# Weights masked on VectorE instead of ScalarE, and products with v moved behind the transposes, in a fused attention and feed-forward kernel

## The chip, the cores and the metric

The kernel runs on one core of one Trainium2 chip. The metric is the device time of a whole execution in microseconds (us), as the median of several. TensorE multiplies matrices (its weight loads are listed apart), VectorE, ScalarE and GpSimd do the element-wise work, and SyncE issues most transfers. The profile calls them PE, PEld, DVE, ACT, POOL and SP.

## The reference

```python
# q, k, v: (8, 8, 576, 64) float32; tau = 0.02
scores = np.matmul(q, k.transpose(0, 1, 3, 2)) / 8
thresh = scores.max(-1, keepdims=True) - tau
scores = np.where(scores >= thresh, scores, -1e9)
attn = np.exp(scores - scores.max(-1, keepdims=True))
attn = attn / (attn.sum(-1, keepdims=True) + 1e-9)
x = heads_joined(np.matmul(attn, v))                  # (8, 576, 512)
xn = (x - x.mean(-1)) / np.sqrt(x.var(-1) + 1e-6) * g_ln
out = x + np.maximum(xn @ w_ch1, 0) @ w_ch2           # w: 512x2048 and 2048x512
```

(cut; the keepdims of the second block are left out.) The weights come in 64-bit floating point and are made into 32-bit ones on the chip.

## The kernel before

The work is a chain of 160 steps. Eight batches have four pairs of heads each, and a pair has five steps (places 0 to 4 in the pair): four with 128 rows of each head, one with the last 64 rows of both. A step is: scores on TensorE, row maximum on VectorE (`neg`), threshold on GpSimd (`thr`), exponential on ScalarE, mask by the threshold and row sum on VectorE (`e`), reciprocal on VectorE (`den`), scaling on GpSimd. A step or two later the weights of attention are transposed and multiplied with v (`pv`). In the first batch (steps 0 to 19) TensorE transposes; in the others VectorE transposes 32x32 blocks (`et`), a transfer writes them to DRAM (`scr`) and another fetches them back in the right order (`em`).

Up to step 27 the kernel also converts the weights, one chunk of 128x512 a step and two in steps 20 to 23. The bits of a chunk are put together in `a`; `y` is a factor that is 0 where the weight is too small for a 32-bit number, and otherwise 1 or the feature's g:

```python
nc.scalar.activation(y, high_words_as_f32, func=AF.Square)
gh = half_sb if gi is None else g_half[:, gi : gi + 1]
nc.scalar.activation(y, y, func=AF.Sign, bias=tiny_sb)
nc.scalar.activation(y, y, func=AF.Identity, scale=gh, bias=gh)
...                                                   # in the next step:
nc.gpsimd.tensor_tensor(out=chunks[i][0], in0=a, in1=y, op=ALU.mult)
```

From step 25 on the feed-forward products of the batch before (`p`, 2304 matmuls in all) fill the time between the attention steps. The transposes and the order of the first batch:

```python
def turn_weights(u, j, es):
    ...
    tr = ps_at.tile([128, 2, 128], F32, tag="at", name="tr")   # two PSUM buffers "at"
    for h in range(2):
        tp = pool.tile([128, J, 128], F32, tag=tag, name="tp") # "at" for h == 0
        ...                              # 4 transposes into tp, then em <- tp on ScalarE
    for h in range(2):
        ...
        nc.vector.tensor_copy(er[r, o : o + 128], tr[r, h])    # the last 64 rows

at_point(3 * n + 3, turn_weights, u, j, es)      # next step, behind its scores
if j in (1, 3, 4):                               # the step after, ahead of its transposes
    at_point(3 * n + 6, lambda u=u, j=j: values_of(u, j, rounds.pop(u)))
```

`values_of` takes an "at" buffer for the products with v and copies the result to `x` on ScalarE. In the batches 1 to 7 it is called at `3 * n + 12`, four steps after the scores.

Of the kernel before, what the change touches and what calls it, by code (L numbers as in the profile page):

```python
# [8 lines left out]
F32 = mybir.dt.float32  # L9
# [3 lines left out]
ALU = mybir.AluOpType  # L13
AF = mybir.ActivationFunctionType
# [4 lines left out]
def kernel(  # L19
# [25 lines left out]
    nc = tc.nc  # L45
# [5 lines left out]
    NK = DM // 128  # L51
# [11 lines left out]
    consts = ctx.enter_context(tc.tile_pool(name="consts", bufs=1))  # L63
# [13 lines left out]
    low_sb = consts.tile([128, 1], F32, name="low_sb")  # L77
    eps_sb = consts.tile([128, 1], F32, name="eps_sb")
    g_sb = consts.tile([128, NK], F32, name="g_sb")
    g_half = consts.tile([128, NK], F32, name="g_half")  # L80
    half_sb = consts.tile([128, 1], F32, name="half_sb")
    tiny_sb = consts.tile([128, 1], F32, name="tiny_sb")
    ident = consts.tile([128, 128], F32, name="ident")
    avg_sb = consts.tile([128, 128], F32, name="avg_sb")
    w1_sb = [consts.tile([128, DF], F32, name=f"w1_{i}") for i in range(NK)]
# [26 lines left out]
    def load_v(u):  # L112
# [13 lines left out]
        out=tau_sb, in_=bass.AP(tensor=tau.tensor, offset=tau.offset, ap=[[0, 128], [1, 1]])  # L126
# [3 lines left out]
    for t in q_diag:  # L130
# [3 lines left out]
    make_identity(nc, ident)  # L134
    nc.vector.memset(eps_sb, 1e-6)
    nc.vector.memset(avg_sb, 1.0 / DM)
    nc.vector.memset(half_sb, 0.5)
    nc.vector.memset(tiny_sb, -(1.0625 * 2.0**-15) ** 2)



# [1 line left out]
        out=scl_sb, in0=tau_sb, scalar1=0.0, scalar2=SCALE, op0=ALU.is_ge, op1=ALU.mult  # L143
    )
    nc.vector.tensor_scalar(
        out=low_sb, in0=tau_sb, scalar1=0.0, scalar2=BIG, op0=ALU.is_lt, op1=ALU.mult
    )
    nc.vector.scalar_tensor_tensor(
        out=low_sb, in0=tau_sb, scalar=-1.0, in1=low_sb, op0=ALU.mult, op1=ALU.subtract
    )  # L150
    nc.gpsimd.dma_start(out=g_sb, in_=g_ln.rearrange("(c p) -> p c", p=128))
    nc.gpsimd.tensor_scalar(
        out=g_half, in0=g_sb, scalar1=0.5, scalar2=1.0, op0=ALU.mult, op1=ALU.mult
    )

    WC = 512

# [2 lines left out]
    def weight_steps(which):  # L160










        if which == 1:
            chunks = [
                (w1_sb[i][:, c : c + WC], w_ch1[i * 128 : (i + 1) * 128, c : c + WC], i)
                for c in range(0, DF, WC)
                for i in range(NK)
            ]
        else:
            chunks = [
                (w2_sb[i], w_ch2[i * 128 : (i + 1) * 128, :], None) for i in range(ND)
            ]  # L180
        size = len(chunks)
        step = 4 if which == 1 else 2
        place = [ND - step * ((i % 4 if which == 1 or i < size - 4 else i % 2) + 1) for i in range(size)]
        raws, made = {}, {}

        def fetch_raw(i):
            at = place[i]
            raws[i] = hidden[:, at : at + 2].rearrange("p a n -> p (a n)").bitcast(I64)
            nc.sync.dma_start(out=raws[i], in_=chunks[i][1])

        def begin(i):
            if which == 1:
                a, y = hidden[:, place[i] + 2], hidden[:, place[i] + 3]
            else:
                a = ffn.tile([128, WC], F32, tag="o", name="w_bits")
                y = ffn.tile([128, WC], F32, tag="o", name="w_size")
            raw = raws.pop(i)
            words = raw.bitcast(U32).rearrange("p (n two) -> p n two", two=2)
            lo, hi = words[:, :, 0], words[:, :, 1]
            r = raw.bitcast(I32).rearrange("p (n two) -> p n two", two=2)[:, :, 0]  # L200
            au = a.bitcast(U32)
            nc.vector.tensor_scalar(
                out=au, in0=hi, scalar1=3, scalar2=0x3FFFFFFF,
                op0=ALU.logical_shift_left, op1=ALU.bitwise_and,
            )
            nc.vector.scalar_tensor_tensor(
                out=au, in0=hi, scalar=0xC0000000, in1=au,
                op0=ALU.bitwise_and, op1=ALU.bitwise_or,
            )
            nc.scalar.activation(r, lo, func=AF.Copy, scale=2.0**-29)  # L210
            nc.scalar.activation(
                y, raw.bitcast(F32).rearrange("p (n two) -> p n two", two=2)[:, :, 1],
                func=AF.Square,
            )
            gi = chunks[i][2]
            gh = half_sb if gi is None else g_half[:, gi : gi + 1]
            nc.scalar.activation(y, y, func=AF.Sign, bias=tiny_sb)
            nc.scalar.activation(y, y, func=AF.Identity, scale=gh, bias=gh)
            made[i] = (a, y, r)

        def carry(i):
            a, y, r = made[i]
            ai = a.bitcast(I32)
            nc.gpsimd.tensor_tensor(out=ai, in0=ai, in1=r, op=ALU.add)
            if place[i] in place[i + 1 :]:
                fetch_raw(place.index(place[i], i + 1))

        def end(i):
            a, y, r = made.pop(i)
            nc.gpsimd.tensor_tensor(out=chunks[i][0], in0=a, in1=y, op=ALU.mult)  # L230

        return size, lambda: [fetch_raw(place.index(at)) for at in sorted(set(place), reverse=True)], begin, carry, end

    def by_blocks(u):

        return units[u][0] > 0
# [83 lines left out]
    rounds = {}  # L320

    def turn_weights(u, j, es):


        if j in (0, 2, 4):
            n = 256 if j < J else 64
            em = att.tile([128, 2, J, 256], F32, tag="em", name="em")
            er = att.tile([128, 256], F32, tag="er", name="er")
            rounds[u] = (em, er, n)
        em, er, n = rounds[u]  # L330
        tr = ps_at.tile([128, 2, 128], F32, tag="at", name="tr")
        for h in range(2):
            e = es[:, h] if j < J else es[:, 0]
            if j < J or h == 0:
                pool, tag = (ps_at, "at") if h == 0 else (ps_ff, "ff")
                tp = pool.tile([128, J, 128], F32, tag=tag, name="tp")
                for c in range(J):
                    nc.tensor.transpose(tp[:, c], e[:, c * 128 : (c + 1) * 128], ident)  # L338
                if j < J:
                    o = (j % 2) * 128  # L340
                    nc.scalar.copy(em[:, h, :, o : o + 128], tp)
                else:
                    nc.scalar.copy(
                        em[:, :, :, :64], tp.rearrange("p c (h t) -> p h c t", h=2)
                    )
            if h == 0:
                nc.tensor.transpose(tr[:64, 0], e[:, 512:576], ident)
            else:
                nc.tensor.transpose(tr[:, 1], e[:, 448:576], ident)
        for h in range(2):  # L350
            r = slice(64 * h, 64 * h + 64)
            if j < J:
                o = (j % 2) * 128
                nc.vector.tensor_copy(er[r, o : o + 128], tr[r, h])
            else:
                nc.vector.tensor_copy(er[r, :64], tr[r, h, r])

    def turn_blocks(u, j, es):

# [102 lines left out]
    def run_aside():  # L462
        now = aside[:]
        aside.clear()
        for fn in now:
            fn()
# [124 lines left out]
    def at_point(n, fn, *args):  # L591
        later_calls.setdefault(n, []).append((fn, args))

    def run(n):
        for fn, args in later_calls.pop(n, ()):
            fn(*args)
# [47 lines left out]
    n = 0  # L644
    for u in range(len(units)):
        for j in range(PTS):
            blocks = by_blocks(u)
            scs = scores(u, j)
            es, thr = exponentials(scs)
            conversion.carry()  # L650
            run(3 * n)
            second_part(n, 0)
            weights(scs, es, thr)
            run_aside()
            conversion.end()
            run(3 * n + 1)
            second_part(n, 1)
            if j == 2 and u + 1 < len(units):
                turn(u + 1)
            if j == 3 and u + 2 < len(units):  # L660
                load_qk(u + 2)
            if j == 4 and 0 < u < len(units) - 1:
                load_v(u + 1)
            conversion.begin(2 if 20 <= n < 24 else 1)
            if blocks:
                box = []
                at_point(3 * n + 4, lambda u=u, j=j, es=es, box=box: box.append(turn_blocks(u, j, es)))
                if j in (1, 3, 4):
                    at_point(3 * n + 7, lambda j=j, box=box: box.append(fetch(j, box[0])))
                    at_point(3 * n + 12, lambda u=u, j=j, box=box: values_of(u, j, box[1]))  # L670
            else:
                at_point(3 * n + 3, turn_weights, u, j, es)
                if j in (1, 3, 4):
                    at_point(3 * n + 6, lambda u=u, j=j: values_of(u, j, rounds.pop(u)))
            n += 1
    while later_calls or queue or aside:
        run(3 * n)
# [35 lines left out]
```

## Time and profile before

| | |
|---|---|
| median of 3 executions | 1567.52 us (1562.31 to 1567.53) |
| profiled execution | 1561.5 us, mean granted clock 0.965 |
| PE busy | 95% of the span |
| VectorE, ScalarE, GpSimd busy | 52%, 30%, 33% |

The prediction shows the views that it rests on. Four more lines of the page of before turn out to matter. The first is the chain that ended last, by engine. The second is the group of the products with v: busy time and mean ns of one, then the idle time of TensorE just before them and what ended it. The last two are transfers: count, KB each, and median us from issue to landing.

```profile
PE 79%; SPq 6%; DVE 5%; DMA 4%; POOL 2%; ACT 2%; issue 2%; POOLq 0%; DVEq 0%; ACTq 0%
...
L416 PE MATMUL pv<-em,v_in 128*64 128x256 f32 (+1 forms) x1536 | 167.1, 353 | 6.1 <-DMA em<-scr 5.9
...
scr<-et SPq DMA_DIRECT2D x224, 288.0 KB, 4.4
em<-scr SPq DMA_DIRECT2D x112, 512.0 KB, 5.0
```

The products with v lose only 6.1 us to waiting, so the fetch of `em` looks harmless. But it is there (5.9 us), in the dense part of the kernel, where TensorE is the bound, and 10% of the chain (SP's queue and DMA) are transfers.

### The profile page before, as it was taken

To read this page: it belongs to the slowest core of one execution; us is meant where nothing else is said; L and a number is where in the kernel's file an instruction comes from. 1 tells how busy PE (TensorE), PEld (TensorE's weight loads), DVE (VectorE), ACT (ScalarE), POOL (GpSimd) and SP (SyncE) were. 2 spreads that over 40 slices of the span, in tenths; PEclk is the share of its full clock that TensorE was granted. 3 is DMA by queue.
4 is the path that set the end of the run, shared out by engine and by line. 5 is a ranking of instruction groups with operands and counts; after the bars stand their busy time and mean duration, and the time that the engine had idled before them with its cause. 6 is when DMAs were issued, how large, how long until landed. Compare 5 with 4: busy or idle time off the path is not lost.

```text
span 1561.5 us, 17868 instructions
## 1 busy us (share of the span) xinstructions
PE 1477.1 (95%) x5686; PEld 714.8 (46%) x5686; DVE 808.6 (52%) x1548; ACT 460.8 (30%) x786; POOL 513.9 (33%) x774
## 2 busy tenths in 40 slices
PE   5777699999999999999999999999999999999998
PEld 3444344444444444444444444444444444444443
DVE  5666676666556655665566555655656551001001
ACT  5666664212321232123211421133113320210200
POOL 4656673333223322333233323332333222100000
PEclk8867599999999999999999999999999999999999
DMA  5333387787667776777667767776777665001001
GB/s 141 96 87 94 106 199 165 166 182 163 152 156 173 165 167 152 161 152 190 141 150 167 162 156 159 157 174 150 159 154 169 149 139 121 7 3 17 7 7 20
DMA packets 701452, 204.37 MB, mean 131 GB/s; under 512 B 632752, under 2 KB 697264, under 8 KB 701360
## 3 DMA queue, kind: packets, MB, share of 16 engines
q1 hardware_dynamic: 698960, 202.95, 57.1%
q8 instruction: 46, 0.75, 0.2%
q10 hardware_dynamic: 2368, 0.30, 0.1%
q14 instruction: 46, 0.38, 0.1%
q0 software_dynamic: 32, 0.00, 0.0%
HBM read 119.41 MB, written 83.76 MB: 130 GB/s over the span
## 4 chain that ended last, share of the span: by engine, by line
PE 79%; SPq 6%; DVE 5%; DMA 4%; POOL 2%; ACT 2%; issue 2%; POOLq 0%; DVEq 0%; ACTq 0%
PE p L494 31%; PE p L536 26%; PE pv L416 10%; PE sc L278 10%; DMA em<-scr 4%; DVE e L309 2%; SPq L103 2%; SPq L479 1%; SPq L372 1%; ACT e L297 1%; PE tp L338 1%; SPq L117 1%; DVE neg L290 1%; SPq L121 1%; POOL w L230 1%
## 5 line engine op out<-in xcount | busy, mean ns | idle before, releaser
L494 PE MATMUL p<-xc,w 128*128 128x512 f32 x1152 | 518.6, 600 | 12.5 <-DVE xc L455 9.8
L536 PE MATMUL p<-hidden,w 128*128 128x512 f32 x1152 | 513.1, 597 | 0.0
L297 ACT ACTIVATE e<-sc,neg 128x576 f32<-128x576 f32 x288 | 199.9, 737 | 602.7 <-DVE neg L290 588.5
L290 DVE TENSOR_REDUCE neg<-sc 128x1 f32<-128x576 f32 x288 | 206.2, 751 | 309.7 <-PE sc L278 309.0
L494 PEld LDWEIGHTS p<-xc,w 128*128 128x128 f32 x1152 | 213.1, 190 | 270.0 <-issue 244.9
L536 PEld LDWEIGHTS p<-hidden,w 128*128 128x128 f32 x1152 | 214.2, 190 | 263.2 <-issue 260.5
L315 POOL TENSOR_SCALAR e<-e,den 128x576 f32<-128x576 f32 x288 | 218.3, 764 | 257.1 <-DVE den L313 241.1
L309 DVE SCALAR_TENSOR_TENSOR e<-sc,thr,e 128x576 f32<-128x576 f32 x288 | 225.4, 816 | 70.4 <-ACT e L297 69.0
L293 POOL TENSOR_SCALAR thr<-neg,low_sb 128x1 f32<-128x1 f32 x288 | 76.0, 264 | 501.2 <-DVE neg L290 500.3
L278 PE MATMUL sc<-kT,qT 64*128 64x288 f32 x1024 | 188.3, 459 | 39.4 <-DVE e L309 30.9
L501 ACT ACTIVATE hidden<-p 128x512 f32<-128x512 f32 x144 | 86.0, 598 | 352.6 <-PE p L494 352.5
L416 PE MATMUL pv<-em,v_in 128*64 128x256 f32 (+1 forms) x1536 | 167.1, 353 | 6.1 <-DMA em<-scr 5.9
L278 PEld LDWEIGHTS sc<-kT,qT 64*128 64x128 f32 x1024 | 103.2, 198 | 148.8 <-issue 93.7
L365 DVE STREAM_TRANSPOSE et<-e 128x1152 f32<-128x1152 f32 x112 | 152.9, 1365 | 0.5
L416 PEld LDWEIGHTS pv<-em,v_in 128*64 128x64 f32 x1536 | 93.6, 145 | 85.4 <-issue 43.4
L471 POOL TENSOR_TENSOR o<-o,x 128x512 f32<-128x512 f32 x36 | 45.7, 1268 | 216.5 <-DVE o L470 216.5
L470 DVE TENSOR_TENSOR o<-p,rb 128x512 f32<-128x512 f32 x36 | 24.6, 683 | 161.5 <-PE p L536 150.0
L416 PE MATMUL pv<-er,v_rest 128*64 128x256 f32 (+1 forms) x384 | 54.3, 332 | 0.0
L510 POOL TENSOR_TENSOR ss<-ss,sq 128x512 f32<-128x512 f32 x27 | 34.4, 1273 | 60.1 <-ACT sq L508 60.1
L427 ACT COPY x<-pv 128x256 f32<-128x256 f32 (+3 forms) x120 | 32.0, 288 | 46.3 <-PE pv L416 42.9
L278 PE MATMUL sc<-kT,q_diag 128*128 128x288 f32 x128 | 37.7, 418 | 6.3 <-DVE e L309 6.2
L255 DVE STREAM_TRANSPOSE qT<-q_in 128x256 f32<-128x256 f32 x56 | 21.6, 423 | 41.6 <-POOL q_in L248 41.6
(68 smaller groups left out, 694.6 us busy)
## 6 DMA issues: line engine op xcount, KB each, us to landing
scr<-et SPq DMA_DIRECT2D x224, 288.0 KB, 4.4
em<-scr SPq DMA_DIRECT2D x112, 512.0 KB, 5.0
hidden<-in_moe_w_ch_dram SPq DMA_DIRECT2D x32, 512.0 KB, 3.8
q_in<-in_q_dram SPq DMA_DIRECT2D x128, 72.0 KB, 4.3
out_dram<-ot SPq DMA_DIRECT2D x144, 64.0 KB, 1.9
k_in<-in_k_dram SPq DMA_DIRECT2D x124, 72.0 KB, 2.6
v_in<-in_v_dram SPq DMA_DIRECT2D x64, 128.0 KB, 3.6
scr_rest<-et SPq DMA_DIRECT2D x112, 72.0 KB, 4.6
```

Of the source, the lines that this page charges most:

```text
L278: nc.tensor.matmul(sc[:, c, :HALF], lhsT=lhsT, rhs=kT[rows, c * HALF : (c + 1) * HALF], start=True, stop=True,)
L290: nc.vector.tensor_reduce(out=neg[:, i : i + 1], in_=sc[:, :, :HALF], axis=AXL.XY, op=ALU.max, negate=True)
L293: nc.gpsimd.tensor_scalar(out=thr[:, i : i + 1], in0=neg[:, i : i + 1], scalar1=-1.0, scalar2=low_sb, op0=ALU.mult, op1=ALU.add,)
L297: nc.scalar.activation(es[:, i].rearrange("p (c n) -> p c n", c=2), sc[:, :, :HALF], func=AF.Exp, bias=neg[:, i : i + 1],)
L309: nc.vector.scalar_tensor_tensor(out=e2, in0=sc[:, :, :HALF], scalar=thr[:, i : i + 1], in1=e2, op0=ALU.is_ge, op1=ALU.mult, accum_out=den ...
L315: nc.gpsimd.tensor_scalar(out=es[:, i], in0=es[:, i], scalar1=den[:, i : i + 1], scalar2=1.0, op0=ALU.mult, op1=ALU.mult,)
L365: nc.vector.transpose(et[:, :, :, j % 2], es.rearrange("p h (n c) -> p h n c", c=32))
L416: nc.tensor.matmul(pv[64 * h : 64 * h + 64, :n], lhsT=vt[:, c, h, :] if c < J else vr[:, h, :], rhs=em[:, h, c, :n] if c < J else er[:, :n ...
L471: nc.gpsimd.tensor_tensor(out=o, in0=o, in1=groups[g][:, m], op=ALU.add)
L494: nc.tensor.matmul(p1, lhsT=w1_sb[c][:, d * 128 : (d + 1) * 128], rhs=xc[:, c, :], start=(c == 0), stop=(c == NK - 1),)
L501: nc.scalar.activation(hidden[:, d], p1, func=AF.Relu)
L536: nc.tensor.matmul(p2, lhsT=w2_sb[d][:, m * 128 : (m + 1) * 128], rhs=hidden[:, d], start=(d == 0), stop=(d == ND - 1),)
```

## The change

The intent: ScalarE's two operations Sign and Identity go, as does GpSimd's multiplication. VectorE does test and multiplication in one instruction. GpSimd then scales by g, for the first matrix only. In the first batch the products with v are issued half a step later, behind the transposes, and the `er` copies go to ScalarE.

```diff
-    g_half = consts.tile([128, NK], F32, name="g_half")
-    half_sb = consts.tile([128, 1], F32, name="half_sb")
-    tiny_sb = consts.tile([128, 1], F32, name="tiny_sb")
 ...
-            gi = chunks[i][2]
-            gh = half_sb if gi is None else g_half[:, gi : gi + 1]
-            nc.scalar.activation(y, y, func=AF.Sign, bias=tiny_sb)
-            nc.scalar.activation(y, y, func=AF.Identity, scale=gh, bias=gh)
 ...
-            nc.gpsimd.tensor_tensor(out=chunks[i][0], in0=a, in1=y, op=ALU.mult)
+            dst, _, gi = chunks[i]
+            nc.vector.scalar_tensor_tensor(
+                out=dst if gi is None else a, in0=y, scalar=(1.0625 * 2.0**-15) ** 2, in1=a,
+                op0=ALU.is_ge, op1=ALU.mult,
+            )
+            if gi is not None:
+                nc.gpsimd.tensor_scalar(
+                    out=dst, in0=a, scalar1=g_sb[:, gi : gi + 1], scalar2=1.0,
+                    op0=ALU.mult, op1=ALU.mult,
+                )
 ...
-                nc.vector.tensor_copy(er[r, o : o + 128], tr[r, h])
+                nc.scalar.copy(er[r, o : o + 128], tr[r, h])
 ...
-                    at_point(3 * n + 6, lambda u=u, j=j: values_of(u, j, rounds.pop(u)))
+                    at_point(3 * n + 7, lambda u=u, j=j, tw=rounds_at: values_of(u, j, tw[0]))
```

(cut: the filling of the removed constants, the other `er` copy, the list that carries `em` and `er` to the later point.)

More of the change, by code (lines that the diff above doesn't have):

```diff
@@ L136 @@
     nc.vector.memset(avg_sb, 1.0 / DM)
-    nc.vector.memset(half_sb, 0.5)
-    nc.vector.memset(tiny_sb, -(1.0625 * 2.0**-15) ** 2)
     nc.vector.tensor_scalar(
@@ L151 @@
     nc.gpsimd.dma_start(out=g_sb, in_=g_ln.rearrange("(c p) -> p c", p=128))
-    nc.gpsimd.tensor_scalar(
-        out=g_half, in0=g_sb, scalar1=0.5, scalar2=1.0, op0=ALU.mult, op1=ALU.mult
-    )
     WC = 512
@@ L353, in turn_weights @@
                 o = (j % 2) * 128
-                nc.vector.tensor_copy(er[r, o : o + 128], tr[r, h])
+                nc.scalar.copy(er[r, o : o + 128], tr[r, h])
             else:
-                nc.vector.tensor_copy(er[r, :64], tr[r, h, r])
+                nc.scalar.copy(er[r, :64], tr[r, h, r])
+        return em, er, n
     def turn_blocks(u, j, es):
@@ L671 @@
             else:
-                at_point(3 * n + 3, turn_weights, u, j, es)
+                rounds_at = []
+                at_point(
+                    3 * n + 3,
+                    lambda u=u, j=j, es=es, tw=rounds_at: tw.append(turn_weights(u, j, es)),
+                )
                 if j in (1, 3, 4):
-                    at_point(3 * n + 6, lambda u=u, j=j: values_of(u, j, rounds.pop(u)))
+                    at_point(3 * n + 7, lambda u=u, j=j, tw=rounds_at: values_of(u, j, tw[0]))
             n += 1
```

## The prediction

> **What bounds the kernel now.** I read the busy shares by slices of the span first, then stretches cut at the first score reduction of each pair of heads, then the chain that ended last in order of time, then the order of instructions inside single steps.
>
> The page, busy tenths in 40 slices of 39 us, and the granted clock in tenths:
>
> ```profile
> PE   5777699999999999999999999999999999999998
> PEclk8867599999999999999999999999999999999999
> ```
>
> After slice 5 (about 200 us) TensorE is busy nine tenths or more at full clock; only the first 200 us are loose. The same as stretches (PE, PEld, DVE, ACT, POOL busy us, clock, DMA share, GB/s), one pair of heads of the first batch each, then the steps in which two chunks of weights are converted, then the beginning of the dense part:
>
> ```profile
> 44.80:81.20 36.40, 26.36 (x141) 16.11 (x138) 25.45 (x58) 25.15 (x42) 23.89 (x30) 0.78 0.35 91
> 81.20:122.20 41.00, 31.11 (x150) 19.04 (x150) 25.86 (x58) 24.96 (x42) 25.16 (x31) 0.70 0.33 90
> 122.20:159.50 37.30, 27.27 (x139) 17.18 (x136) 25.43 (x58) 25.23 (x42) 24.97 (x31) 0.74 0.32 90
> 159.50:215.00 55.50, 38.43 (x132) 18.40 (x132) 38.09 (x67) 33.92 (x54) 36.28 (x40) 0.68 0.53 143
> 215.00:260.00 45.00, 45.00 (x193) 21.87 (x190) 31.65 (x59) 26.64 (x45) 25.47 (x34) 1.00 0.79 183
> ```
>
> Before 215 us no engine is full, so the limit there is a cycle of waits. After it PE is full, so what is won before 215 us stays won and what is won after it is worth nothing. All that the change touches (32 chunks in steps 0 to 27, the transposes in steps 1 to 20) lies before about 240 us. The chain that ended last shows the cycle in one step (start, us, what):
>
> ```profile
> 88.42 3.02 PE sc L278 x8
> 91.44 1.26 PE pv L416 x20
> 92.70 1.05 PE tp L338 x4
> 93.97 0.85 PE tp L338 x4
> 95.36 0.29 DVE er L354
> 95.69 0.84 DVE e L309 x2
> 96.57 3.02 PE sc L278 x8
> ```
>
> Scores, then the previous products with v, then the previous transposes, then VectorE's copy of the last rows (er). Only behind that copy, in VectorE's order, stands the mask (L309), and it frees the PSUM tile that the next scores need. The exponentials had long ended. In a step that turns q and k it is another chain, and in the double steps a third (timeline, with what ended the idle time):
>
> ```profile
> 63.18 1.47 POOL L315 TENSOR_SCALAR e<-e,den 128x576 f32<-128x576 f32 x2 [1.00 <-DVE den L313]
> 64.61 1.27 POOL L230 TENSOR_TENSOR w<-hidden 128x512 f32<-128x512 f32 x1
> 65.85 0.75 POOL L248 TENSOR_SCALAR q_in<-q_in,scl_sb 128x576 f32<-128x576 f32 x1
> 66.64 0.71 DVE L259 STREAM_TRANSPOSE qT<-q_in 128x512 f32<-128x512 f32 x1 [2.84 <-POOL q_in L248]
> 180.37 1.48 DVE L202 TENSOR_SCALAR w_bits<-hidden 128x512 uint32<-128x512 uint32 x1 [3.24 <-POOL w L230]
> ```
>
> GpSimd multiplies the weight (1.27 us) before it scales q, and VectorE waits 2.84 us for q. At 180 us VectorE waits 3.24 us because GpSimd's multiplication still holds the chunk's two buffers.
>
> **What the Trainium skill says.** "TensorE: Matmul & The Clock Gate", Part 1, has the array at half clock after an idle window of about 3.4 us and at full clock after a busy one. The trace agrees: four score products take 3.02 us at 88 us, where the clock is 0.50, and 1.24 us at 228 us, where it is 1.00; the v products take 4.15 or 2.31 us. "SBUF — State Buffer", Who interferes with whom, says that VectorE with two SBUF inputs, or in a two-port mode, and GpSimd exclude each other for a whole instruction. The trace agrees: L206 (two inputs) takes 0.69 us alone and 1.11 beside L315, and L202 took 1.48 instead of 0.41 while L230 ran. "GPSIMD Engine Reference", Engine selection, has two-input operations about twice as slow there as on VectorE and one-input ones near line rate; here 1.27 us for L230 with two inputs, 0.74 for L315 with one.
>
> **The change part by part.** (a) Per chunk ScalarE loses Sign (0.72) and Identity (0.81): 1.53 us, 32 times, 49 us of busy time. ScalarE was 25 of 37 us busy and rarely last, so of this almost nothing is on the path, save about 1 us of waiting ahead of the exponentials in three of the double steps. (b) GpSimd loses the multiplication of 1.27 us, 32 times; 16 chunks of the first matrix get a one-input scaling by g, which I estimate at 0.70 from L315 (0.74 for 576 columns). (c) VectorE gains 32 masks of the size and kind of L206, 0.69 alone. It loses 32 copies er of 0.29 and 8 of 0.22, together 11 us, which go to ScalarE.
>
> The place of (c) matters more than its size. The mask stands right behind the reciprocal and takes the shared ports first, so the scaling of e (two of 0.74), L202 and L206 come after it in turns: 0.69 + 0.74 + 0.41 + 0.74 + 0.69 = 3.3 us from reciprocal to next reduction, where before it was 1.55. This is the price of the change, some 1.7 us in each plain step.
>
> (d) With er off VectorE, the first step shows what a step without that copy takes: reduction at 10.78, reciprocal ended at 14.20, i.e. 3.42 us. So VectorE's floor is 3.42 + 3.3 = 6.7 us a step with two heads' rows, about 5.4 in the single-tile step.
>
> (e) The transposes ahead of the v products: these now take the PSUM buffer of the first transposes, so they wait for the em copy that empties it. That copy stands behind the exponentials on ScalarE: reduction + 2.2 (reduction 0.85, two exponentials 1.37) + 0.6. So the v products begin 2.9 us after the reduction, and the next scores stand behind them. With cold products (4.15) and about 1.2 us until the next reduction this makes 8.3 us; warm 2.9 + 2.3 + 1.2 = 6.4, and then VectorE's floor of 6.7 holds.
>
> Now a pair of heads, from reduction to reduction. Before: the mean of the three pairs between 44.84 and 159.52. Place in the pair, before, after:
> - 0 (v products): 7.6; 7.6 (between 6.7 and 8.3, as the clock is mixed).
> - 1 (small v products): 7.4; 6.7 (VectorE's floor).
> - 2 (turning): 11.0; 9.2. Reciprocal ends at 3.4; mask 0.7, scaling e 1.5, g 0.7 (second matrix: none), scaling q 0.75, then qT and the diagonal 1.2, L202 and L206 1.1: 9.4 and 8.7.
> - 3 (v products after idle time, cold): 7.2; 7.9, worse, for in the kernel before they ran in the shadow of the turning, and now behind the exponentials.
> - 4 (single tile): 5.0; 5.4.
> Sum 38.2 before, 36.8 after: 1.4 us a pair, some 4 for three pairs, and about nothing for the first, which ran warm (34.1).
>
> The double steps 20 to 24 took 12.6, 11.4, 12.4, 10.2 and 8.8 us, 55.4 together. Freed from GpSimd's multiplication: step 20 becomes 8.3 (cold v products); step 21: exponentials 1 us late behind ScalarE's chunk operations, two masks, one 32x32 transpose of 1.36 and two chunks, 10.4; step 22: VectorE is nearly full already (centring 2.46, turning), and two masks make it 13.0; step 23: no wait of 2.34 us but two masks, 9.0; step 24: TensorE's work at full clock, 8.2. Sum 48.9: 6.5 us.
>
> Together 4 + 6.5 = 10.5 us, taken as 12 because shorter idle gaps may warm the array a little: 1567.5 - 12 = 1555.
>
> **The rivals.** First, the array becomes warm throughout the first batch: then place 0 takes 6.7 and place 3 the same (6.7), 2.1 us less for each of four pairs, and with shorter scores perhaps 1 more; some 1543. For it speaks that PE then has fewer gaps per step; against it that at place 3 the v products still come after 3.5 us or more of idle time, and that steps with only 1.5 us of gap (88 to 104 us) stayed cold. Second, VectorE does not alternate with GpSimd so badly (the mask beside the scaling costs 0.69 and nothing else shifts): plain steps then fall to 5.7, and I get 1 us for places 1, 2 and 4 each, 12 us over four pairs; again about 1543. Third, the v products behind the exponentials always run cold and ScalarE, with er and the copy to x in front of the next chunk, delays the next exponentials: 8.3 at places 0 and 3 and a us more at place 1, which eats 2 us a pair; some 1563. Fourth, a transfer that is hidden anyway: chunks are fetched four ahead and no wait for them is in the chain, so I give this nothing.
>
> **Range and chances.** All gains lie in 205 us, where VectorE's floors (6.7, 6.7, 9.2, 6.7, 5.4, together 34.7 a pair) allow three times 3.5 and the 6.5 of the double steps, 17 us at best; 2% is 31 us. So faster by over 2% needs two rivals together: 0.06. Slower by over 2% needs each of the first 21 steps to lose 1.5 us: 0.02. Same: 0.92. The three times before already differ by 5 us, so the range is 1539 to 1567.
>
> **What would show it.** Right: the dense part of PE begins at about 203 us instead of 215 and the rest has equal length; the mask L309 begins about 1.65 us after the reduction everywhere; idle time of VectorE on GpSimd's weight operation is gone; the v products of places 0 and 3 wait for em; the weight mask takes about 0.69 and the next L202 about 1 us. Wrong: the clock over 44 to 160 us rises from 0.74 to above 0.9 (first rival), the reduction follows the reciprocal within 2.2 us (second), or place 0 exceeds 8.5 us (third).

## The result, and the profile after

The changed kernel took 1573.14 us (median of 4, 1571.76 to 1573.66) against 1567.53 for the kernel before beside it. The ratio is 1.0041, with a 95% interval of 1.0017 to 1.0065. Ratios here are the mean time of one kernel's runs over that of the other's runs of the same rounds, so they are not quite the ratio of the medians. All outputs are right. The change loses 0.4%, where I had predicted a gain of 0.8%; the time lies outside my range (1539 to 1567).

The slices of the page of after, as those that open the prediction:

```profile
PE   5667699989999999999999999999999999999998
...
PEclk8787899999999999999999999999999999999999
```

The dense part begins in the sixth slice as before, but the slice ahead of it ran at a clock of 0.8 and not 0.5. And in PE's row an 8 stands in the ninth slice (314 to 353 us), well in the dense part. The stretches, cut at the reductions as before (the first pair that answers to 44.80:81.20, the double steps, and 45 us behind them; PE, PEld, DVE, ACT, POOL busy us, clock, DMA share, GB/s):

```profile
43.70:80.00 36.30, 25.34 (x145) 15.53 (x144) 25.38 (x53) 19.24 (x41) 23.20 (x30) 0.76 0.37 89
...
151.48:197.08 45.60, 29.75 (x131) 14.20 (x130) 43.09 (x73) 20.72 (x37) 28.57 (x30) 0.85 0.58 155
197.08:242.08 45.00, 41.44 (x174) 20.42 (x171) 32.02 (x59) 21.34 (x36) 19.68 (x27) 0.96 0.76 176
```

Step 25 begins at 197.08 and not at 214.91, the double steps took 45.6 us and not 55.4. So the beginning won more than predicted. But behind it PE is busy 41.44 of 45 us, where before it had all 45.

To see where the gain went I listed the reciprocal of each of the 160 steps in both traces and took the difference, after minus before:

| step | 0 | 5 | 10 | 15 | 20 | 26 | 28 | 43 | 83 | 103 | 128 | 159 |
|---|---|---|---|---|---|---|---|---|---|---|---|---|
| us | +1.3 | -2.9 | -5.9 | -9.1 | -12.8 | -19.4 | -13.7 | -7.1 | -1.9 | +0.1 | +3.5 | +7.7 |

The change wins 19.4 us up to step 26, and 27.1 us are lost from there on, although nothing was changed there. (1.3 us of both are no more than a late reciprocal: in the kernel before, that of step 26 came 4.5 us after its reduction and not 3.2, and step 27 gives it back.) The time is lost at steps 27 to 29 and then mostly at two places in each batch; between these jumps the steps of the two kernels have equal length. From step 28 on nearly every jump stands behind products with v that wait for a freshly fetched `em` (25.5 us in 20 waits). The chain of after at the jump of step 43 (start, us, what):

```profile
328.88 5.24 DMA em<-scr
...
334.16 3.95 PE pv L414 x18
338.11 3.63 PE p L534 x8
```

The products with v stand behind the transfer, and after the pause they run cold: at 3.95 us and not at 2.37, with a granted clock of 0.59 over these 3.95 us where it was 1.00 before. The same lines of the page as shown of before:

```profile
PE 78%; DVE 8%; DMA 6%; SPq 4%; ACT 2%; issue 1%; POOL 1%; POOLq 0%; ACTq 0%; DVEq 0%
...
L414 PE MATMUL pv<-em,v_in 128*64 128x256 f32 (+1 forms) x1536 | 171.0, 353 | 56.5 <-DMA em<-scr 25.5
...
scr<-et SPq DMA_DIRECT2D x224, 288.0 KB, 5.0
em<-scr SPq DMA_DIRECT2D x112, 512.0 KB, 5.1
```

Waiting for `em` rose from 5.9 to 25.5 us (of the other 31 of the 56.5 us, 29 are the wait for the copy `em` in the first batch, which the new order brings and the prediction expected). Above all, the same transfers take longer: `scr<-et` lands after 5.0 us and not 4.4. For `q_in` it is 5.0 and not 4.3. No instruction that issues them was touched.

What differs is where the tiles lie. Each of the three removed constants took 32 bytes of every SBUF partition, so every tile that is allocated after them moved down by 96 bytes. The compiled program lists the addresses: `et` from 163200 to 163104, `em` from 144768 to 144672, `q_in` from 118144 to 118048. In the kernel before, all large tiles start 128 bytes behind a multiple of 256 ("128 mod 256"); in the changed kernel, 32 behind one. That gives two suspects: the addresses, and the change of work itself.

### The profile page after: what moved, and what is told of

It is laid out like the page before. It is cut to its first block, busy times and chain, and to the rows that moved or that the text cites. A ratio compares the mean times of both kernels' runs of the same rounds, so it can differ in the third digit from the quotient of the medians.

```text
span 1570.0 us, 17831 instructions
## 1 busy us (share of the span) xinstructions
PE 1462.5 (93%) x5686; PEld 710.3 (45%) x5686; DVE 815.9 (52%) x1538; ACT 420.5 (27%) x762; POOL 498.2 (32%) x757
## 4 chain that ended last, share of the span: by engine, by line
PE 78%; DVE 8%; DMA 6%; SPq 4%; ACT 2%; issue 1%; POOL 1%; POOLq 0%; ACTq 0%; DVEq 0%
PE p L534 29%; PE p L492 27%; PE pv L414 11%; PE sc L275 9%; DMA em<-scr 5%; DVE neg L287 2%; SPq L477 2%; DVE e L306 2%; ACT e L294 1%; DVE w_bits L198 1%; DVE hidden L198 1%; SPq L396 1%; DVE et L363 0%; DVE w L219 0%; SPq L392 0%
## 5 line engine op out<-in xcount | busy, mean ns | idle before, releaser
L534 PE MATMUL p<-hidden,w 128*128 128x512 f32 x1152 | 513.1, 598 | 0.0
L312 POOL TENSOR_SCALAR e<-e,den 128x576 f32<-128x576 f32 x288 | 232.1, 812 | 226.4 <-DVE den L310 208.9
L414 PE MATMUL pv<-em,v_in 128*64 128x256 f32 (+1 forms) x1536 | 171.0, 353 | 56.5 <-DMA em<-scr 25.5
L275 PE MATMUL sc<-kT,qT 64*128 64x288 f32 x1024 | 172.9, 441 | 26.3 <-DVE e L306 16.5
L275 PEld LDWEIGHTS sc<-kT,qT 64*128 64x128 f32 x1024 | 95.6, 191 | 131.2 <-issue 89.0
L469 POOL TENSOR_TENSOR o<-o,x 128x512 f32<-128x512 f32 x36 | 45.7, 1269 | 216.2 <-DVE o L468 216.2
L414 PE MATMUL pv<-er,v_rest 128*64 128x256 f32 (+1 forms) x384 | 59.0, 343 | 0.0
L508 POOL TENSOR_TENSOR ss<-ss,sq 128x512 f32<-128x512 f32 x27 | 34.4, 1274 | 66.5 <-ACT sq L506 66.5
```

The source lines that it names most:

```text
L275: nc.tensor.matmul(sc[:, c, :HALF], lhsT=lhsT, rhs=kT[rows, c * HALF : (c + 1) * HALF], start=True, stop=True,)
L312: nc.gpsimd.tensor_scalar(out=es[:, i], in0=es[:, i], scalar1=den[:, i : i + 1], scalar2=1.0, op0=ALU.mult, op1=ALU.mult,)
L414: nc.tensor.matmul(pv[64 * h : 64 * h + 64, :n], lhsT=vt[:, c, h, :] if c < J else vr[:, h, :], rhs=em[:, h, c, :n] if c < J else er[:, :n ...
L469: nc.gpsimd.tensor_tensor(out=o, in0=o, in1=groups[g][:, m], op=ALU.add)
L534: nc.tensor.matmul(p2, lhsT=w2_sb[d][:, m * 128 : (m + 1) * 128], rhs=hidden[:, d], start=(d == 0), stop=(d == ND - 1),)
```

## The experiments

In the table "addresses" is the place of the large tiles mod 256, and each call's kernels ran on one chip with the kernel before beside them (its medians: 1564.58, 1561.58, 1560.15 and 1561.94 us, seven runs each). The four calls ran on four chips, on which the median of the same kernel before differs by 4 us (it was 1567.53 in the call of the result), so runs of different calls are better compared by their ratios than by their medians.

| run | addresses | median us | ratio to before, 95% interval |
|---|---|---|---|
| after_pad96 | 128 | 1547.00 | 0.9885 (0.9865 to 0.9904) |
| before_late | 32 | 1587.60 | 1.0143 (1.0124 to 1.0162) |
| after_pad32 | 64 | 1567.83 | 1.0018 (1.0002 to 1.0035) |
| after_res0 | 0 | 1530.71 | 0.9783 (0.9766 to 0.9800) |
| before_res0 | 0 | 1549.80 | 0.9922 (0.9902 to 0.9942) |
| mask_only | 128 | 1572.17 | 1.0064 (1.0039 to 1.0089) |
| order_only | 128 | 1561.99 | 0.9999 (0.9982 to 1.0016) |
| after_later | 32 | 1555.45 | 0.9957 (0.9937 to 0.9977) |
| er_vector | 128 | 1542.79 | 0.9886 (0.9855 to 0.9917) |
| v_old_place | 128 | 1530.19 | 0.9792 (0.9761 to 0.9824) |
| after_in128_att0 | 128 and 0 | 1530.66 | 0.9809 (0.9775 to 0.9842) |
| res0_place3 | 0 | 1523.56 | 0.9754 (0.9725 to 0.9783) |
| v_old_own_addresses | 32 | 1555.04 | 0.9956 (0.9928 to 0.9984) |
| v_old_res0 | 0 | 1513.01 | 0.9689 (0.9662 to 0.9715) |
| v_old_res0_later | 0 | 1526.62 | 0.9774 (0.9748 to 0.9801) |
| v_mixed_res0 | 0 | 1514.07 | 0.9692 (0.9661 to 0.9724) |

### The addresses alone

Four kernels change no work, only addresses.

after_pad96, the changed kernel with the removed bytes put back:

```diff
+    pads = [consts.tile([128, 1], F32, name=f"pad{i}") for i in range(3)]
     ident = consts.tile([128, 128], F32, name="ident")
```

> The changed kernel with three unused 32-byte tiles in the place of the three constants that the change removed, so that every later SBUF tile starts where it started in the kernel before; no instruction differs. Layout theory (the transfers of 128- and 256-byte pieces became slower because all tiles moved down by 96 bytes, from a start of 128 modulo 256 to one of 32): scr<-et lands in 4.4 us at the median instead of 5.0, k_in in 2.6 instead of 3.2, the start gets back 1.3 us, and the 19 us that the compute has won by step 26 are for the most part kept: 1549 to 1556 us. Phase theory (the earlier compute makes transfers collide, and the address has nothing to do with it): 1573 us within 3 and landing times as in the changed kernel.

before_late, the kernel before with the three constants behind all other tiles (their lines in `consts` go):

```diff
     ffn = ctx.enter_context(tc.tile_pool(name="ffn", bufs=4))
+    late = ctx.enter_context(tc.tile_pool(name="late", bufs=1))
+    g_half = late.tile([128, 4], F32, name="g_half")
+    half_sb = late.tile([128, 1], F32, name="half_sb")
+    tiny_sb = late.tile([128, 1], F32, name="tiny_sb")
```

> The kernel before with its three small constants in a pool of their own behind all others, so that every other tile starts 96 bytes lower, as in the changed kernel; no instruction differs. Layout theory: scr<-et 5.0 us, k_in 3.2 us, and the time grows by as much as the padding takes from the changed kernel, to 1580 to 1592 us. Phase theory: 1567 us within 3, scr<-et 4.4 us.

after_pad32, as after_pad96 with one unused tile:

```diff
+    pads = [consts.tile([128, 1], F32, name=f"pad{i}") for i in range(1)]
```

> The changed kernel with one unused 32-byte tile: tiles start at 64 modulo 256. If what matters is a multiple of 64 bytes, transfers and time are as with three tiles (1549 to 1556 us); if it is 128 bytes, as without (1573 us) or in between. Phase theory: 1573 us.

after_res0, the changed kernel with one constant moved behind all others:

```diff
-    eps_sb = consts.tile([128, 1], F32, name="eps_sb")
+    late = ctx.enter_context(tc.tile_pool(name="late", bufs=1))
+    eps_sb = late.tile([128, 1], F32, name="eps_sb")
```

> The changed kernel with one 32-byte constant moved behind all other pools: tiles start at 0 modulo 256. If only 64 or 128 bytes matter, as with three padding tiles; if 256 bytes matter, scr<-et and v_in, whose pieces have 256 bytes, land faster still (under 4.2 us) and the time is 2 to 8 us below that of three tiles. Phase theory: 1573 us.

With three unused tiles, 96 bytes that nothing reads or writes, the changed kernel falls from 1573.1 to 1547.0 us. The kernel before, moved by the same 96 bytes, rises from 1564.6 to 1587.6. So the layout is a cause of its own, and it is larger than the change: 26 us for the one kernel (1.6% by the ratios), 23 for the other (1.4%). At equal addresses the change is worth a gain of 1.15%. One unused tile (64 mod 256) brings little, 1567.8, so a multiple of 64 is not enough. At multiples of 256 the changed kernel is at 1530.7, faster than at any other place, and 16 us below three tiles where I had expected 2 to 8. The landing times go with it. From the page of after_pad96:

```profile
scr<-et SPq DMA_DIRECT2D x224, 288.0 KB, 4.5
em<-scr SPq DMA_DIRECT2D x112, 512.0 KB, 4.9
```

At 0, 128, 64 and 32 mod 256, `scr<-et` lands after 4.2, 4.5, 5.0 and 5.0 us in the changed kernel, and `q_in` after 4.1, 4.2, 4.9 and 5.0. The wait of the products with v for `em` is 1.0, 9.3, 23.6 and 25.5 us. The durations of the engines' instructions in the dense part do not change (`p` takes 601 ns at all four). The kernel before, moved by 96 bytes, waits for `em` as the changed kernel does, and not 5.9 us (engine and what it waited for: us in total, times, longest):

```profile
PE pv L417 <- DMA em<-scr: 21.4, 18, 2.4
```

The reciprocals divide the 27.1 us that were lost behind step 26. With 96 bytes put back 5.0 us of it remain and 22 are gone. The jump of step 43, shown above, is not among those 22: it is 4.7 us in after_pad96, by the change alone, and 4.7 us in before_late, by the addresses alone. The addresses make most of the others.

The pieces of `et` that a transfer moves are 256 bytes, those of q and k 128, those of `em` 1024. The Trainium skill, "DMA: Bandwidth & Descriptors", How a descriptor splits into AXI transactions, says that a transaction must start at a multiple of 256 bytes and that a piece that does not start there pays for bytes it does not use. The runs agree that a multiple of 256 is the best of the four places tried. They don't agree with the order that follows from the page's count of 32-byte beats: for a 256-byte piece I estimate from it 8 beats at 0, 9 at 32, 10 at 64 and 12 at 128, so 128 should be the worst, but for `scr<-et` it is the second best. The pieces of q lie 128 bytes apart and so start at two places in turn; there the same count makes 6, 6, 8 and 7 beats on the mean at 0, 128, 64 and 32, and that nearly fits the landings of `q_in`.

before_res0 does for the kernel before what after_res0 did for the changed one: `eps_sb` and the three constants go to the pool `late`.

> The kernel before with four 32-byte constants moved behind all other tiles, so that every large tile starts at a multiple of 256 bytes. If layout and change are two separate causes that add, the layout takes the same 1.05% from the kernel before as it took from the changed one (1547.0 to 1530.7): 1548 us, and the change is worth 1.1% at this layout too. Rival: the late landings only bite behind the faster beginning of the changed kernel; then the kernel before stays near 1562 and the change is worth 2% here.

1549.8, where two separate causes should make 1548. At equal addresses the change gains about the same everywhere, with ratios of ratios 0.9885 at 128, 0.9783 / 0.9922 = 0.986 at 0 and 1.0041 / 1.0143 = 0.990 at 32.

after_in128_att0 has the inputs at 128 and the attention tiles at 0:

```diff
-    tau_sb, scl_sb, low_sb, eps_sb, g_sb            # lines in consts (shortened here)
+    mid = ctx.enter_context(tc.tile_pool(name="mid", bufs=1))   # tau, scl, low, eps
     att = ctx.enter_context(tc.tile_pool(name="att", bufs=2))
+    ...                                             # and g_sb in a pool behind ffn
```

> The changed kernel with the inputs q, k, v and the chunks' buffer at 128 mod 256 and the attention tiles (et, em and all behind them) at a multiple of 256. All at 128 was 1547.0, all at 0 was 1530.7. Theory: the 128-byte pieces of q and k keep within one 256-byte line at both, only the 256-byte pieces of et straddle one, so the attention tiles make the whole difference: 1531. Rival: the v pieces (256 bytes too) or the queue as a whole matter, then in between, about 1539.

1530.66 against 1530.71 with all at 0, on different chips. By the ratios it is 0.9809 against 0.9783, with 0.9885 for all at 128; the intervals of the first two overlap. So most or all of the difference between 128 and 0 comes from the attention tiles and what is allocated behind them (`x` and the feed-forward tiles moved too, so `et` alone is not shown). Between 32 and 128 I have not parted the inputs from the attention tiles.

### Is it the wait for em?

after_later leaves the bad addresses and gives the products with v of the batches 1 to 7 half a step more.

```diff
-                    at_point(3 * n + 12, lambda u=u, j=j, box=box: values_of(u, j, box[1]))
+                    at_point(3 * n + 13, lambda u=u, j=j, box=box: values_of(u, j, box[1]))
```

> The changed kernel as it is, at its unfavourable addresses, only that in the batches 1 to 7 the products with v are issued half a step (about 3.9 us) later, with the transfers at their old place. If the unfavourable addresses cost time only because the products with v wait for em, 1573 falls to about 1548 and the idle time of the v products on em from 25 us to under 5. Rival: late landings also hold up the SP queue and the buffers, so the wait only moves to another place: 1565 or more.

1555.45: 17.7 us of the 26 come back at unchanged addresses (13 by the ratios), and the wait on the transfer falls from 25.5 us to this:

```profile
PE pv L414 <- DMA em<-scr: 7.3, 5, 3.1
```

Both numbers I gave for the theory (1548, under 5 us) were too good. A later run shows one reason: at good addresses the same edit costs 13.6 us (v_old_res0_later below), and its sign, a longer busy time of `p` (530.1 and 523.5 us), is in this trace too. So the wait was worth more than what came back.

### The parts of the change, at the addresses of the kernel before

mask_only: the masks without the new order and with `er` on VectorE (three unused tiles). order_only: the kernel before with the new order and `er` on ScalarE; it allocates the same tiles as before.

```diff
 # mask_only, against the changed kernel
-                nc.scalar.copy(er[r, o : o + 128], tr[r, h])
+                nc.vector.tensor_copy(er[r, o : o + 128], tr[r, h])
-                    at_point(3 * n + 7, lambda u=u, j=j, tw=rounds_at: values_of(u, j, tw[0]))
+                    at_point(3 * n + 6, lambda u=u, j=j: values_of(u, j, rounds.pop(u)))
 # order_only: these two edits the other way round, against the kernel before
```

> The masking of the weights on VectorE alone, at the addresses of the kernel before (three unused tiles): er copies stay on VectorE, products with v stay ahead of the transposes. My theory gives most of the 17.6 us that both parts won at these addresses to the double steps (8.6) and to the steps that turn q and k, which are freed of GpSimd's multiplication: about 1554 us. Rival: the masks stand in VectorE's way as long as the er copies are still there, and most of the gain is the order's: 1560 or more.

> The new order in the first batch and er on ScalarE alone; weights by Sign and Identity as in the kernel before; same addresses. My theory: the plain steps win (er no longer between the products with v and the mask of e), place 3 loses about 1 us a pair: 1559 us, so that the two parts add to the 17.6 us. Rival: behind ScalarE's four operations a chunk the er copies come late and the order is worth nothing without the masks: 1565, within 0.2% of the kernel before.

Both theories fell, and both rivals came true in their numbers. The masks alone are 0.6% slower, the order alone is worth nothing, together they gain 1.15%. Here are the steps of the first batch, as means of the pairs 1 to 3 from reduction to reduction, and the double steps 20 to 24 together. The last two rows are the next two runs (one trace each):

| kernel (128 mod 256) | place 0 | 1 | 2 | 3 | 4 | pair | steps 20 to 24 |
|---|---|---|---|---|---|---|---|
| before | 7.6 | 7.4 | 11.0 | 7.2 | 5.0 | 38.2 | 55.4 |
| predicted for the change | 7.6 | 6.7 | 9.2 | 7.9 | 5.4 | 36.8 | 48.9 |
| after_pad96: all of it | 6.3 | 5.4 | 9.6 | 8.5 | 4.6 | 34.4 | 46.8 |
| mask_only | 9.4 | 7.8 | 10.3 | 7.7 | 5.7 | 40.8 | 49.9 |
| order_only | 8.3 | 6.5 | 10.0 | 8.7 | 4.8 | 38.2 | 53.7 |
| er_vector: order, er on VectorE | 5.5 | 5.8 | 9.7 | 8.2 | 4.7 | 33.9 | 45.7 |
| v_old_place: er on ScalarE, old order | 5.4 | 6.1 | 8.8 | 5.8 | 4.6 | 30.7 | 45.8 |

A plain step of mask_only, place 1, in the chain that ended last:

```profile
99.27 0.11 ACT x L426
...
99.42 0.30 PE tr L345
99.72 0.44 PE tp L336 x4
...
100.60 0.29 DVE er L352
...
100.93 1.58 DVE e L307 x4
```

The products with v hold an "at" buffer until ScalarE has copied them to `x`, behind its exponentials. Only then come the last transposes, then VectorE's `er`, and behind that in VectorE's order the mask of e. So VectorE stands still in the middle of its step (1.84 us before `er` in this one), and the weight mask of 0.67 us comes on top of a cycle that runs through VectorE anyhow. TensorE's gaps become longer too: the clock from 44 to 160 us was 0.68, and 0.74 in the kernel before.

A step of order_only in the same view:

```profile
96.02 1.16 POOL e L315
97.18 1.24 POOL w L230
98.42 0.23 POOL sum L442
...
99.64 0.27 POOL thr L293
...
99.94 0.04 DVE e L309
```

With `er` off VectorE, its mask waits for the threshold, which GpSimd computes behind its weight multiplication (`w`, which the masks would have removed) and a sum. Places 1 and 2 win 0.9 us each against the kernel before, but places 0 and 3 lose 0.7 and 1.5, where the products with v now wait for `em`. So each part alone leaves a wait that only the other removes.

er_vector and v_old_place divide the second part. They are the changed kernel with three unused tiles:

```diff
 # er_vector
-                nc.scalar.copy(er[r, o : o + 128], tr[r, h])
+                nc.vector.tensor_copy(er[r, o : o + 128], tr[r, h])
 # v_old_place
-                    at_point(3 * n + 7, lambda u=u, j=j, tw=rounds_at: values_of(u, j, tw[0]))
+                    at_point(3 * n + 6, lambda u=u, j=j: values_of(u, j, rounds.pop(u)))
```

> The changed kernel at the addresses of the kernel before (three unused tiles), with only the er copies put back on VectorE; masks on VectorE and the new order stay. Both parts together were worth 17.6 us (1547), masks alone cost 10 (1572). Theory: what makes the masks pay is that VectorE's queue no longer stops at er for the transposes; then er on VectorE, even in the new order, holds the mask of e back and plain steps are 7.5 us instead of 5.4: near 1562. Rival: the order does it, since with the v products behind the transposes er is ready early; then 1550.

> The other half: the changed kernel at the addresses of the kernel before, er on ScalarE, but the products with v ahead of the transposes as before. Theory (er on ScalarE is what makes the masks pay): within 3 us of 1547, and place 3 back at 7.2 us instead of 8.3 to 9.0. Rival: the order does it: about 1565, er coming late behind the cold products.

The rival was near for er_vector and the theory had the direction for v_old_place, but that either edit is enough, neither had. With the order alone beside the masks it is 1542.8 (0.9886), so `er` on VectorE does no harm behind early transposes. With `er` on ScalarE alone beside the masks it is 1530.2 (0.9792). And with both it is 1547.0 (0.9885): given `er` on ScalarE, the reordering costs 16.8 us by the medians of two chips, and 15 by the ratios. Either edit frees VectorE from the wait for the late transposes, so doing the second after the first wins nothing more. What is left of the reordering is its price, the wait of the products with v for `em`. Place 3 shows it. The changed kernel, products with v in the timeline of TensorE (start, us, what, idle time before and what ended it):

```profile
69.19 3.68 PE L414 MATMUL pv<-em,v_in 128*64 128x256 f32 x16 [4.25 <-ACT em L338]
72.66 1.07 PE L414 MATMUL pv<-er,v_rest 128*64 128x256 f32 x4
```

The same place in v_old_place:

```profile
87.29 1.95 PE L415 MATMUL pv<-em,v_in 128*64 128x256 f32 x16
89.06 0.60 PE L415 MATMUL pv<-er,v_rest 128*64 128x256 f32 x4
```

There they run without a wait in all four pairs, while VectorE and GpSimd turn q and k, and warm in two of them (2.38 us for all 20; 4.46 and 4.06 in the others). The idle time comes after them, where nothing stands behind it. In the changed kernel they wait 3.1 to 4.6 us in all four pairs and then take 3.9 to 4.5 us. Place 3 takes 5.8 us and not 8.5.

res0_place3 undid the order for place 3 only, at multiples of 256:

```diff
-                    at_point(3 * n + 7, lambda ...)
+                    at_point(3 * n + (6 if j == 1 else 7), lambda ...)
```

> A try for the best kernel: all large tiles at a multiple of 256 (1530.7), and in the first batch only the products of place 3 back at their old place ahead of the transposes, since place 3 went from 7.2 to between 8.3 and 9.0 us. If they run in the shadow of the turning again, 1 us in each of four pairs: 1526. Rival: they then run cold or keep the transposes and with them em and er back, and the next step loses what this one wins: 1531 or a little more.

1523.56, 7 us less than after_res0 on another chip; by the ratios (0.9754 against 0.9783) it is the expected 5. Place 3 fell from 8.6 to 5.4 us, but place 0 rose from 6.3 to 7.4 (means of the pairs 1 to 3), as its products with v ran cold in two of them.

### Do the two causes add?

By then one thing was open: whether order and addresses are two causes. v_old_own_addresses is the changed kernel with only the order undone, at its own addresses. v_old_res0 is the same with `eps_sb` moved behind all other tiles.

> The changed kernel at its own addresses (32 mod 256), with only the order of the first batch undone. If the two causes add: 1530.2 + 26.1 = 1556, that is, the whole change without the reordering would have gained 0.4% even at its bad addresses. Rival (partly one cause): the lost time after step 26 depends on how early the dense part begins, then anything from 1530 to 1545 or over 1562.

> Old order, er on ScalarE, masks on VectorE, all large tiles at a multiple of 256. If the two causes add: 1530.2 - 16.3 = 1514. If they overlap: 1520 or more.

1555.0 and 1513.0, where sums gave 1556 and 1514. They add, by the ratios too (0.9792 x 1.0041 / 0.9885 = 0.9946 against 0.9956, and 0.9792 x 0.9783 / 0.9885 = 0.9691 against 0.9689):

| median us | 128 mod 256 | 32 mod 256 | 0 mod 256 |
|---|---|---|---|
| kernel before | 1560 to 1568 | 1587.6 | 1549.8 |
| the change | 1547.0 | 1573.1 | 1530.7 |
| the change with the old order | 1530.2 | 1555.0 | 1513.0 |

v_old_res0 is 3.1% faster than the kernel before and the best of all, with 2.6 us of waiting for `em` left. From its page:

```profile
L415 PE MATMUL pv<-em,v_in 128*64 128x256 f32 (+1 forms) x1536 | 154.2, 341 | 2.6 <-DMA em<-scr 2.6
...
scr<-et SPq DMA_DIRECT2D x224, 288.0 KB, 4.2
```

Two attempts to better it failed. v_old_res0_later adds the edit of after_later (12 to 13). v_mixed_res0 has the new order for the small products of place 1 only:

```diff
-                    at_point(3 * n + 6, lambda ...)
+                    at_point(3 * n + (7 if j == J else 6), lambda ...)
```

> The same, and in the batches 1 to 7 the products with v issued half a step later. If no wait for em is left at these addresses, the time stays within 3 us of the run before it; if late landings still cost something there, up to 5 us less.

> As v_old_res0, but the small products with v (64 columns, place 1) behind the transposes as in the changed kernel, where place 1 took 5.4 us against 6.2: 2 us less than v_old_res0. Rival: as in the run with only place 3 undone, place 0 then goes back to 7.9 us for the array is cold there, and it is 5 us slower.

The first is 13.6 us slower with no wait for `em` left at all. The two groups of feed-forward products are busy 530.1 and 523.5 us in it and not 518.6 and 513.1. Why they take longer, no run settles. The second is within 1.1 us of v_old_res0, neither the 2 us of the theory nor the 5 of the rival: place 1 in the pairs 1 to 3 is 0.6 us quicker, place 2 is 0.8 slower.

## Why the prediction was wrong

**The step that failed** is that "what is won before 215 us stays won", or as "what would show it" has it, "the rest has equal length", together with the fourth rival, "a transfer that is hidden anyway", to which I gave nothing. I looked for a wait for the weights' chunks and found none, but I did not ask whether the change touches the transfers of the dense part. The step table shows 27.1 us lost there, nearly all in jumps at `em`, and 22 of them by the addresses. The address runs show the cause: with the 96 bytes put back the time is 1547.0, inside the range and 8 us under the point. The hint was on the page of before: 5.9 us of waiting for `em` where TensorE is the bound, and in the diff three tiles that are gone.

**Mis-sized: the price of the mask.** I had VectorE and GpSimd alternate strictly and put 3.3 us between reciprocal and next reduction. VectorE in the changed kernel, one step (start, us, what):

```profile
89.61 0.17 DVE L310 RECIPROCAL den<-den 128x2 f32<-128x2 f32 x1
89.69 0.67 DVE L219 SCALAR_TENSOR_TENSOR hidden<-hidden 128x512 f32<-128x512 f32 x1
90.28 0.42 DVE L194 TENSOR_SCALAR hidden<-hidden 128x512 uint32<-128x512 uint32 x1
90.73 1.03 DVE L198 SCALAR_TENSOR_TENSOR hidden<-hidden 128x512 uint32<-128x512 uint32 x1
91.69 1.41 DVE L287 TENSOR_REDUCE neg<-sc 128x1 f32<-128x576 f32 x2
```

Counted as the 1.55 of before was, from the reciprocal's successor (89.69) to the reduction (91.69), it is 2.0 us. VectorE ran the mask and L194 in a row at 0.67 and 0.42 us; the one that waits, as I read it, is GpSimd, whose pair of scalings beside them takes 2.40 us and not 1.47. That wait was not the last one there. The second rival was the right one. The floor of a plain step is 5.4 us and not 6.7.

**The other steps.** In the reading of the clock, 0.50 holds only from 89.09 us on: over the scores at 88.42 it was 0.61. Those at 96.57, of the same 3.02 us, ran at 0.50, so the conclusion stands. (a) ScalarE's 49 us less and the `er` copies of 11 us that it takes over give 38; its busy time fell from 460.8 to 420.5. (b) The scaling by g was estimated at 0.70 us and took 0.69. GpSimd fell by 15.7 us and not by the 29 that 32 x 1.27 less 16 x 0.70 makes; the scaling of e grew from 764 to 812 ns in 288 instructions, 13.8 us. (e) The products with v of places 0 and 3 begin 2.7 us after the reduction (46.43 after 43.70, 69.19 after 66.44; predicted 2.9), and place 0 takes 8.4 cold and 6.3 warm (predicted 8.3 and 6.4). That place 3 gets worse was right, too mildly (8.5 at equal addresses, predicted 7.9). (d) That `er` off VectorE lowers its floor is shown by v_old_place against mask_only, 42 us. But I took the change as one piece and did not see that it had two remedies for one wait, of which the second, the new order, only costs.

**The sum.** At equal addresses the beginning won 21.4 us up to the first reduction of step 26, where I had 12: 11.4 in the pairs 1 to 3 (predicted 4), 8.6 in the double steps (6.5), 1.2 in the first pair (0), and 0.2 in step 25. Of this 3.7 us net were given back behind it, also at the addresses of before; the jump at `em` of step 43 alone is 4.7. I read this as the transfers not moving forward with the rest; what supports it is that at multiples of 256 (after_res0 against before_res0), where they land sooner, none is given back.

**The chances.** The class was right: at 1.0041 the kernel is within 2%. That something outside the working could cost 26 us, more than all the terms in it, was not in the range.

## What to carry to other kernels

When a change adds or removes even one small tile, compare the addresses of the tiles that transfers read and write, mod 256, before you believe a difference of 2%; unused tiles that restore them tell the change from the layout in one run. Here, putting the large tiles at multiples of 256 won about as much as the change (0.8 to 1.0% against 1.15%), and moving them to 32 cost more than the change wins (1.4 to 1.6%). Test the parts of a change in all combinations: two remedies for the same wait need not add, and the second can keep only its cost. And read a small wait on a transfer in the stage that sets the end as a warning that its room may be used up, not as proof that it is hidden.

## What the Trainium skill lacked or had wrong

- "DMA: Bandwidth & Descriptors", How a descriptor splits into AXI transactions: that a start at a multiple of 256 bytes is best agrees, but for `scr<-et` the cost of the other starts does not follow the beats. For its pieces of 256 bytes read from SBUF the landing took 4.2 us at 0, 4.5 at 128, 5.0 at 64 and 5.0 at 32 mod 256, where the beats (8, 12, 10, 9, my estimate from the page) make 128 the worst. The pieces of `q_in`, 128 bytes written to SBUF, took 4.1, 4.2, 4.9 and 5.0, nearly as the count has it. Those of `v_in`, 256 bytes written, show no order (3.5, 3.2, 3.4, 3.6). Landing times include waiting in the queue, so these are no costs of one piece.
- "SBUF — State Buffer", Operand start alignment: it asks for a multiple of the element size only and says it is about what is allowed, not about speed. A line that the start address of tiles filled by transfers can cost 2.6% (a ratio to the kernel before of 1.0041 against 0.9783) is missing there, as is one that a 32-byte constant moves all tiles behind it.
- "SBUF — State Buffer", Who interferes with whom: it says that whoever issues first holds the lock, but not who follows when one engine has been waiting and the other has its next instruction ready. I read alternation into it. Here VectorE ran a mask and L194 back to back (0.67 and 0.42 us) while GpSimd's pair of scalings stretched from 1.47 to 2.40 us.
